# Batch 0 handed from stage to stage on the chip, and weights converted in finer steps

## The chip, the cores and the metric

The kernel runs on one core of a Trainium2 chip. The metric is the device time of one execution in microseconds (us). The engines of the core work in parallel, each through its own queue in order: TensorE (PE) multiplies matrices, VectorE (DVE), ScalarE (ACT) and GpSimd (POOL) work on elements, SyncE (SP) issues transfers (DMAs); ACT and POOL issue transfers too. PEld is PE's weight load, which is the operand that stays in the array. PE writes to an accumulator memory of eight banks (PSUM), which DVE and ACT read.

## The reference

Two blocks follow each other. The first filters the sequence of each batch and channel in the frequency domain, the second is a two-layer network without bias. `x` is 8 x 3008 x 256 in float32. The two weight matrices come as float64.

```python
X = np.fft.rfft(x, axis=1)
Y = X * (filt_r + 1j * filt_i)[None, :, :]
y = np.fft.irfft(Y, n=x.shape[1], axis=1).astype(np.float32)
h = y.reshape(24064, 256) @ w_in          # 256 x 2048
g = h - np.tanh(h)
out = (g @ w_out).astype(np.float32)      # 2048 x 256
```

## The kernel before

**The transform.** 3008 is 64 x 47, and the transform over it is done as products with constant matrices, in three stages per batch. The first stage (`first0` for batch 0, `first` for the others) multiplies 24 pairs of rows of x with `f`: for each pair r, f[r] is the operand that stays in the array and x, 256 channels wide, moves through it. The results are written to a scratch tensor `ct1[b]` in memory and read back in another order by `load_a2`, for the middle stage: that one goes over seven slots (`SLOTS`, five frequencies of 24 rows each, and a last one of two). Per slot it forms two products (`forth`, lines 279 to 294), multiplies by the filter on DVE (`filtered`, 296 to 313), forms the products back (`back`, or `back0` for batch 0), and writes them to a second scratch `ct2[b]`. The last stage (`last`, line 410) reads `ct2` as `e2`, multiplies with `g`, and yields 128 channels x up to 512 tokens, transposed, in `ut`.

**The dense part.** Tokens go in 48 groups (8 batches of 6), the 2048 hidden columns in four quarters: that makes 192 rounds U, four for a group. Round U issues `up(U)` (the product with the quarter of `wu`), in between the steps of `shrink(U - 1)` (h - tanh h, by three ACT activations and DVE products) and of `down(U - 2)` (the product with `wd`). Both products are done in two-by-two blocks with seven products in place of eight, so seven forms of each weight block are kept (`wu` and `wd`, [128, 7, 1024]), of which some are differences (`sums`, line 198, four subtractions on POOL), and the moving operands need differences too: `combine` (line 432), four subtractions, on POOL for nearly all rounds. The round's four sums in h are made on DVE (lines 476, 493, 501, 509), three copies between them on ACT (line 459). The first group of a batch has 448 tokens, so its rounds have 224 columns in place of 256.

**The weights.** float64 cannot be computed with, so each weight is loaded as a pair of 32-bit words (`raw`) and put together again as float32 from its bits. A job (`converted`, line 134) is 128 x 512 numbers; a quarter of `wu` or of `wd` is two jobs and one `sums`. A job is three operations of DVE on the upper word (it, pt, st: mantissa, exponent, sign), two of ACT (ft, pt), one multiply-add with the lower word, the cap of the exponent at 255, the shift into place, and two or three products that write the forms. It is a generator that stops after the load and at four other places. Quarters 0, 1 and 2 of `wu` (six jobs, loaded by POOL's queue) are converted ahead of the dense part, four of the jobs after the first stage of batch 0 and two after its last slot; the other five quarters (wd 0, wu 3, wd 1, 2, 3) in the first dense rounds by `weights_slow`, loaded by SP's queue two jobs ahead, two steps at each of the five calls of `t` in a round.

**The order around the change.** All instructions are in an order written by hand. Before the dense part: the loads of x of batch 0 (SP) and of `f` and `mats` (ACT), the filter rows by POOL (`filters_of`), a small copy `gate` on POOL that waits for the second part of x, and behind it on POOL's queue the loads of the first weights. In the dense part a plan (`planned`, line 937) gives positions to the steps of the transform of the next batches: position 20c + 5u + k is call k of `t` in quarter u of group c. In the first batch `first(1)` is spread over positions 6 to 20, `first(2)` over 20 to 34 (`LEAD`), `middle(1)` over 34 to 104 (`LAG`). `middle` begins with its own loads of a2 and ft, issued when its first step comes. SP's queue also issues the 48 stores of each group's result (`store`, `store_some`).

## Time and profile before

| | us |
|---|---|
| median of 3 runs (2797.88 to 2799.99) | 2798.9 |
| the profiled execution | 2804.2 |
| its span, first to last instruction | 2802.3 |
| PE busy in the span | 2702.2 |
| DVE, ACT, POOL busy | 1682.9, 1735.9, 1375.7 |

The slices on the page are 70 us wide. The first dense round begins at 106.27 us, round 10 at 287.82 us. A record of PE in this float32 kernel is half a matmul: a product is two records. The busy time of an engine says little where its rounds have different limits, so the first 300 us are best read by stretches; from then on PE is busy throughout.

### The profile page before, as it was taken

The page shows a single profiled execution, that of the slowest core. Times are in us where ns is not written, and L with a number is a line of the kernel's source. Part 1 is how long each engine was busy: PE and PEld are TensorE (multiplying, and loading weights), DVE is VectorE, ACT ScalarE, POOL GpSimd, SP SyncE. Part 2 cuts the span into 40 slices and gives each one's busy share as a digit, 9 for nine tenths or more (in the row PEclk, how much of TensorE's full clock was granted, in tenths as well). Part 3 has the DMA queues.
Part 4 walks back from the last instruction along what each step waited for, and adds up shares of the span by engine and source line. Part 5 has one row for each costly group of instructions (what it writes and reads, how often), then busy time and mean ns, then how long its engine had stood idle before and what let it go on. Part 6 is the DMA issues. An engine that isn't in the chain of part 4 may idle for free.

```text
span 2802.3 us, 36449 instructions
## 1 busy us (share of the span) xinstructions
PE 2702.2 (96%) x12878; PEld 2375.4 (85%) x12878; DVE 1682.9 (60%) x2076; ACT 1735.9 (62%) x2603; POOL 1375.7 (49%) x1184
## 2 busy tenths in 40 slices
PE   4888999999999999999999999999999999999998
PEld 3677888988889888988889888898888988899886
DVE  4864775666556665656656666566654766554544
ACT  2455666666666666666666666666666666666665
POOL 4355555544445454545455444454544554454452
PEclk8989999999999999999999999999999999999999
DMA  8655323323132332233223331242322222111110
GB/s 235 196 172 143 76 46 84 86 69 83 50 95 75 88 82 59 69 76 103 55 62 74 102 85 47 61 115 66 78 53 69 53 64 54 30 24 33 21 26 18
DMA packets 341378, 215.44 MB, mean 77 GB/s; under 512 B 227736, under 2 KB 300988, under 8 KB 340995
## 3 DMA queue, kind: packets, MB, share of 16 engines
q1 hardware_dynamic: 295740, 151.00, 22.8%
q10 hardware_dynamic: 40071, 52.71, 6.0%
q0 software_dynamic: 5376, 9.33, 1.2%
q8 instruction: 103, 1.69, 0.2%
q14 instruction: 88, 0.72, 0.1%
HBM read 137.83 MB, written 78.12 MB: 77 GB/s over the span
## 4 chain that ended last, share of the span: by engine, by line
PE 89%; DVE 6%; issue 2%; ACT 2%; DMA 1%; SPq 0%; ACTq 0%; POOL 0%; DVEq 0%
PE o L578 38%; PE x L453 22%; PE z L453 11%; PE y L453 5%; PE pa L287 3%; PE pe L322 3%; PE pu L419 3%; PE pf L255 2%; DVE h L534 1%; DVE h L476 1%; DVE h L509 1%; DMA x<-in_x_dram 1%; DVE xy L312 0%; DVE xy L311 0%; PE pe L803 0%
## 5 line engine op out<-in xcount | busy, mean ns | idle before, releaser
L578 PE MATMUL o<-t,wd 128*128 128x256 f32 (+1 forms) x3072 | 776.5, 375 | 0.0
L433 POOL TENSOR_TENSOR t<-h 128x512 f32<-128x512 f32 (+1 forms) x190 | 261.3, 1375 | 883.9 <-DVE h L534 858.8
L534 DVE TENSOR_TENSOR h<-h,y 128x1024 f32<-128x1024 f32 (+1 forms) x384 | 512.9, 1336 | 287.2 <-ACT y L530 286.7
L578 PEld LDWEIGHTS o<-t,wd 128*128 128x128 f32 x3072 | 584.1, 190 | 70.1 <-issue 2.4
L453 PE MATMUL x<-tu,wu 128*128 128x256 f32 (+1 forms) x2304 | 586.1, 377 | 7.0 <-ACT u L459 6.7
L578 PE MATMUL o<-h,wd 128*128 128x256 f32 (+1 forms) x2304 | 584.3, 376 | 3.0 <-DVE h L534 3.0
L453 PEld LDWEIGHTS x<-tu,wu 128*128 128x128 f32 x2304 | 430.9, 190 | 68.5 <-ACT u L459 15.7
L578 PEld LDWEIGHTS o<-h,wd 128*128 128x128 f32 x2304 | 434.8, 191 | 55.0 <-DVE h L534 4.2
L459 ACT COPY s<-x 128x512 f32<-128x512 f32 (+1 forms) x192 | 110.8, 577 | 508.8 <-PE x L453 497.7
L524 ACT ACTIVATE y<-h 128x1024 f32<-128x1024 f32 (+1 forms) x384 | 400.1, 1042 | 12.8 <-ACT a L256 5.6
L527 ACT ACTIVATE y<-y 128x1024 f32<-128x1024 f32 (+1 forms) x384 | 399.2, 1040 | 12.6 <-ACT a L256 0.4
L530 ACT ACTIVATE y<-y 128x1024 f32<-128x1024 f32 (+1 forms) x384 | 399.9, 1041 | 4.6
L493 DVE TENSOR_TENSOR h<-z,u 128x512 f32<-128x512 f32 (+1 forms) x192 | 130.1, 677 | 267.8 <-ACT u L459 266.6
L459 ACT COPY u<-x 128x512 f32<-128x512 f32 (+1 forms) x384 | 219.3, 571 | 87.8 <-PE x L453 66.2
L435 POOL TENSOR_TENSOR t<-h 128x512 f32<-128x512 f32 (+1 forms) x190 | 271.9, 1431 | 0.0
L434 POOL TENSOR_TENSOR t<-h,t 128x512 f32<-128x512 f32 (+1 forms) x190 | 264.6, 1393 | 14.9
L436 POOL TENSOR_TENSOR t<-t,h 128x512 f32<-128x512 f32 (+1 forms) x190 | 267.6, 1409 | 0.0
L501 DVE COPY h<-x 128x512 f32<-128x512 f32 (+1 forms) x192 | 130.4, 679 | 159.5 <-PE x L453 158.9
L453 PE MATMUL x<-ut,wu 128*128 128x256 f32 (+1 forms) x768 | 195.8, 378 | 1.1 <-DVE h L501 1.1
L453 PE MATMUL z<-tu,wu 128*128 128x256 f32 (+1 forms) x768 | 196.3, 378 | 0.0
L453 PE MATMUL z<-ut,wu 128*128 128x256 f32 (+1 forms) x768 | 195.6, 377 | 0.0
L453 PE MATMUL y<-ut,wu 128*128 128x256 f32 (+1 forms) x768 | 194.9, 376 | 0.0
(118 smaller groups left out, 3068.6 us busy)
## 6 DMA issues: line engine op xcount, KB each, us to landing
e<-ct SPq DMA_DIRECT2D x48, 512.0 KB, 4.2
a<-ct SPq DMA_DIRECT2D x48, 480.0 KB, 5.3
ct<-e ACTq DMA_DIRECT2D x96, 240.0 KB, 2.7
ct<-a ACTq DMA_DIRECT2D x84, 256.0 KB, 2.8
x_sb<-in_x_dram SPq DMA_DIRECT2D x161, 128.0 KB, 3.4
ft<-filt SPq DMA_DIRECT2D x42, 480.0 KB, 6.7
out_dram<-ot SPq DMA_DIRECT2D x1248, 16.0 KB, 1.5
gt<-g SPq DMA_DIRECT2D x48, 256.0 KB, 2.8
```

The lines of the kernel that those rows point to most:

```text
L433: by.tensor_sub(t[0], b[0][1], b[0][0])
L434: by.tensor_sub(t[1], b[1][1], t[0])
L435: by.tensor_sub(t[2], b[1][1], b[0][1])
L436: by.tensor_sub(t[3], t[1], b[1][0])
L453: nc.tensor.matmul(bank[:, k], wu[:, q - 1, (2 * u + k) * 128:(2 * u + k + 1) * 128], rhs[q - 1], start=(first and k == 0), stop=True, ski ...
L459: ACT.copy(t, X)
L501: V.tensor_copy(h[:, 2, :, 0:w], X)
L524: ACT.activation(y[k], ht[k], AF.Arctan, scale=TURN)
L527: ACT.activation(y[k], y[k], AF.Tanh, scale=BEND)
L530: ACT.activation(y[k], y[k], AF.Square, scale=SCALE, accum_out=y_sums[:, 2 * U + k // 2:2 * U + k // 2 + 1])
L534: V.tensor_mul(ht[k], ht[k], y[k])
L578: nc.tensor.matmul(product(q), wd[:, q - 1, (2 * u + k) * 128: (2 * u + k + 1) * 128], rhs[q - 1][:, k], start=(u == 0 and k == 0 and q == ...
```

## The change

Batch 0 no longer passes through `ct1`. Its first products are formed with the two operands exchanged, so that the result has channels on the partitions; ACT copies them into `turnt`, a view of the still empty `wd`. `across` then brings a slot into the layout of the middle stage by eight transposes on PE (product with the identity `one`) and two ACT copies. The identity is loaded early and kept, not in the last round.

The conversion has a stop after each operation; the cap is made by ACT (255 minus the rest, capped at zero from below, and turned back by an exclusive-or), and `sums` is on DVE. Ahead of the dense part the first two weight loads are issued before the filter rows, the next two right after the gate; two jobs are converted before and between the first products, four steps in each slot, the rest behind the last slot. The late quarters begin four loads at a time, a job's first six steps standing ahead of the last steps of the job before; four steps at each `t` and three at each `e`, so 32 in a round. While late weights are pending, `combine` is on DVE. `first(1)` is spread over 2 to 18, `first(2)` over 18 to 34, and `middle(1)` is begun (its first loads issued) at position 27.

```diff
-    def converted(tiles, src, dsts, queue, alone=False):
+    def converted(tiles, src, dsts, queue):
...
         V.tensor_scalar(out=it, in0=hi, scalar1=0xFFFFF, scalar2=None, op0=ALU.bitwise_and)
+        yield
         V.tensor_scalar(out=pt, in0=hi, scalar1=20, scalar2=0x7FF,
                         op0=ALU.logical_shift_right, op1=ALU.bitwise_and)
-        V.tensor_scalar(out=st, in0=hi, scalar1=-2 ** 31, scalar2=None, op0=ALU.bitwise_and)
-        yield
...
+        yield
+        V.tensor_scalar(out=st, in0=hi, scalar1=-2 ** 31, scalar2=0x7F800000,
+                        op0=ALU.bitwise_and, op1=ALU.bitwise_or)
+        yield
+        ACT.activation(ft, it, AF.Identity, bias=1.0, scale=2.0 ** -20)
+        yield
+        ACT.activation(pt, pt, AF.Relu, bias=exp_b)
+        yield
+        ACT.activation(pt, pt, AF.Relu, bias=cap_b, scale=-1.0)
         yield
         V.scalar_tensor_tensor(out=ft, in0=lo, scalar=2.0 ** -52, in1=ft,
                                op0=ALU.mult, op1=ALU.add)
-        V.tensor_scalar_min(pt, pt, 255.0)
         yield
         V.scalar_tensor_tensor(out=pt, in0=pt, scalar=23, in1=st,
-                               op0=ALU.logical_shift_left, op1=ALU.bitwise_or)
+                               op0=ALU.logical_shift_left, op1=ALU.bitwise_xor)
         pt = pt.bitcast(F32)
         for cols, dst, sign in dsts:
+            yield
...
-        G.tensor_sub(w[:, 4], w[:, 6], w[:, 3])
-        G.tensor_sub(w[:, 5], w[:, 4], w[:, 0])
-        G.tensor_sub(w[:, 2], w[:, 1], w[:, 5])
-        G.tensor_sub(w[:, 6], w[:, 0], w[:, 6])
+        for to, one_in, less in ((4, 6, 3), (5, 4, 0), (2, 1, 5), (6, 0, 6)):
+            V.tensor_sub(w[:, to], w[:, one_in], w[:, less])
+            yield
...
+    def late_weights(tiles, quarters):
+
+        jobs = parts_of(quarters)
+        began = [begun(tiles, job) for job in jobs[:4]]
+        yield
+        for k in range(len(jobs) + 1):
+            if k < len(jobs):
+                for _ in range(6):
+                    next(began[k])
+                    yield
+            if k:
+                yield from began[k - 1]
+                if k + 3 < len(jobs):
+                    began.append(begun(tiles, jobs[k + 3]))
+                if k % 2 == 0:
+                    yield from sums(quarters[k // 2 - 1])
+        pending.clear()
...
-        combine(b, [tu[:, k, 0:w] for k in range(4)], G if i else V)
+        combine(b, [tu[:, k, 0:w] for k in range(4)], V if pending else G)
...
-                G if U + 2 < 4 * len(groups) else V)
+                V if pending or U + 2 >= 4 * len(groups) else G)
...
             def first0(xt, c):
 
-                for i in range(2):
-                    r = 8 * c + 4 * i
...
-                            nc.tensor.matmul(pf[:, k], f0[:, r + 2 * j + k],
-                                             xt[:, 4 * i + 2 * j + k], start=True, stop=True)
-                        ACT.copy(a1[:, 2 * j:2 * j + 2, :], pf)
...
-                    ACT.dma_start(dram(ct1[0], r * DM, [[NH * DM, 128], [1, 4 * DM]]), a1)
-                    yield
+                for i in range(4):
+                    r = 8 * c + 2 * i
+                    pf = z0("pf", [128, 2, 2, 128])
+                    for h in range(2):
+                        for k in range(2):
+                            nc.tensor.matmul(pf[:, h, k], xt[:, 2 * i + k, h * 128:h * 128 + 128],
+                                             f0[:, r + k], start=True, stop=True)
+                    ACT.copy(turnt[:, :, :, r:r + 2], pf.rearrange("p h k n -> p h n k"))
+
+            def across(g):
+
+                a, s = SLOTS[g]
+                n = s * NH
+                t = tr.tile([KM, 4, DM], F32, tag="a2", bufs=2, name="a2")
+                for v in (1, 0):
+                    pq = z0("pq", [128, 2, DM])
+                    for k in range(2):
+                        at = (2 * v + k) * NA + a
+                        for h in range(2):
+                            nc.tensor.transpose(
+                                pq[0:n, k, h * 128:h * 128 + 128],
+                                turnt[:, h, at:at + s].rearrange("p a r -> p (a r)"), one)
+                    ACT.copy(t[0:n, 2 * v:2 * v + 2], pq[0:n])
+                return t
...
-                    e1 = tr.tile([KM, 2, DM], F32, tag="e1", bufs=2, name="e1")
+                    e1 = pro.tile([KM, 2, DM], F32, tag="e1", bufs=3, name="e1")
...
+            ACT.dma_start(one, one_d)
             ACT.dma_start(mats, mats_d)
...
+            jobs = parts_of(range(3))
+            began = [begun(tiles0, job, queue=G) for job in jobs[:2]]
             fts = {0: filters_of(0)}
...
-            jobs = parts_of(range(3))
-            began = [begun(tiles0, job, queue=G) for job in jobs[:2]]
+            began += [begun(tiles0, job, queue=G) for job in jobs[2:4]]
             fts[1] = filters_of(1)
-            began += [begun(tiles0, job, queue=G) for job in jobs[2:4]]
...
-            for c in range(3):
-                for _ in first0(xs[c], c):
-                    pass
-            a2 = {0: load_a2(0, 0), 1: load_a2(0, 1)}
-            next(began[0])
-            for k in range(4):
-                convert(k)
+            convert(12)
+            first0(xs[0], 0)
+            convert(14)
+            first0(xs[1], 1)
+            first0(xs[2], 2)
+            a2 = {0: across(0), 1: across(1)}
...
-                    a2[g + 2] = load_a2(0, g + 2)
+                    a2[g + 2] = across(g + 2)
...
                 if g < last_g:
+                    convert(4)
                     back0(g, nn)
...
-                f = [spread(NX, *((6, 20) if b == 1 else (20, LEAD) if b == 2
+                f = [spread(NX, *((2, 18) if b == 1 else (18, LEAD) if b == 2
...
                     next(dw, None)
+                    for _ in range(3):
+                        next(late, None)
...
+                    if i == 1 and pos == LEAD - 7:
+                        mids[1] = middle(1, z1)
+                        next(mids[1])
...
-                    next(late, None)
-                    next(late, None)
+                    for _ in range(4):
+                        next(late, None)
```

More of the change, by code (lines that the diff above doesn't have):

```diff
@@ L119 @@
     exp_b = cst.tile([128, 1], F32, name="exp_b")
+    cap_b = cst.tile([128, 1], F32, name="cap_b")
     groups = [(b, c) for b in range(BATCH) for c in range(NC)]
     count = cst.tile([1, 1], I32, name="count")
+    one = cst.tile([128, 128], F32, name="one_sb")
     def ways(g, back):
@@ L835, with convert @@
             G.tensor_copy(gate, xs[1][0:1, 0, 0:1])
[L836 to L837 removed]
+            began += [begun(tiles0, job, queue=G) for job in jobs[2:4]]
             fts[1] = filters_of(1)
[L839 removed]
             turned_rows()
[L842 to L859 removed]
+            early = weights(tiles0, range(3), G, began)
+            next(early)
+            def convert(n):
+                for _ in range(n):
+                    next(early, None)
+            convert(12)
[4 more added lines that the diff above has]
+            a2 = {0: across(0), 1: across(1)}
             last_g = len(SLOTS) - 1
@@ L890 @@
                     next(fs)
-                    late = weights_slow(tiles1, (4, 3, 5, 6, 7))
+                    signs.clear()
+                    late = late_weights(tiles1, (4, 3, 5, 6, 7))
                     next(late)
             e2s[0] = load_e2(*groups[0])
-            for k in range(4, len(jobs)):
-                convert(k)
+            convert(100)
             warm = z0("warm", [128, 2, 128])
@@ L1007 @@
                     if U == total - 1:
-                        one = tr.tile([128, 128], F32, tag="x", bufs=3, name="one_sb")
-                        nc.sync.dma_start(one, one_d)
                         ones = cst.tile([128, 1], F32, name="ones")
```

84 lines of the change are left out of this document (42 added, 42 removed).

## The prediction

> **What bounds the kernel now.** I read the page first, then the busy time by stretch, then the timeline and the chain of the first 110 us, and last the waits of the first dense rounds.
>
> ```profile
> span 2802.3 us, 36449 instructions
> PE 2702.2 (96%) x12878; PEld 2375.4 (85%) x12878; DVE 1682.9 (60%) x2076; ACT 1735.9 (62%) x2603; POOL 1375.7 (49%) x1184
> PE   4888999999999999999999999999999999999998
> PEclk8989999999999999999999999999999999999999
> ```
>
> A slice is 70 us. From the fifth on PE is full at full clock, and the diff removes no matmul there: 2,500 us are out of reach. What can move lies in the first 260 us. The next two fences are rows of busy time by stretch: start and end, length, then busy time and count for PE, PEld, DVE, ACT and POOL, the granted clock, the DMA share and GB/s. First the stretches before the dense part:
>
> ```profile
> 20.00:30.00 10.00, 8.98 (x34) 7.25 (x33) 0.00 (x0) 2.95 (x6) 5.09 (x9) 1.00 1.07 257
> 30.00:52.69 22.69, 7.20 (x27) 5.48 (x25) 17.07 (x35) 9.36 (x16) 7.90 (x10) 0.70 0.86 289
> 52.69:95.07 42.38, 34.15 (x140) 26.00 (x140) 37.85 (x46) 9.96 (x17) 23.60 (x38) 0.92 0.79 216
> ```
> ```profile
> 40.00:50.00 10.00, 2.29 (x6) 1.80 (x7) 9.86 (x20) 2.82 (x5) 4.23 (x5) 0.50 0.84 234
> ```
> ```profile
> 58.41:64.62 6.21, 6.21 (x15) 4.80 (x16) 5.49 (x7) 0.59 (x1) 6.21 (x12) 0.52 0.53 145
> 64.62:86.00 21.38, 21.27 (x98) 17.04 (x97) 18.11 (x22) 7.04 (x12) 12.00 (x23) 1.00 0.95 247
> ```
>
> Until 30 us the DMA engines are full (share 1.07) and DVE does nothing at all. From 30 to 52.69 DVE converts weights, from 40 to 50 with 9.86 of 10 us busy; from 52.69 to 95.07 it is busy 37.85 of 42.38 us (5.4 per slot) with the filter of batch 0. In the last two rows, parts of the same stretch, PE has no gap: its clock is 0.52 at first, then 1.00, at 21.27/98 = 0.217 us a record. The chain and the timeline say the same:
>
> ```profile
> 2.02 16.12 DMA x<-in_x_dram
> ```
> ```profile
> 28.53 3.69 PE L778 MATMUL pf<-x,f 128*128 128x256 f32 x16 [1.02 <-DMA x<-in_x_dram]
> 40.17 0.42 DVE L145 TENSOR_SCALAR conv<-raw 128x512 int32<-128x512 int32 x1
> 43.64 0.42 DVE L145 TENSOR_SCALAR conv<-raw 128x512 int32<-128x512 int32 x1
> 47.71 5.19 PE L287 MATMUL pa<-a,mats_sb 120*120 120x256 f32 x16 [15.49 <-issue]
> 52.69 0.68 DVE L292 TENSOR_TENSOR xy<-pa,xy 120x512 f32<-120x512 f32 x1
> 94.39 0.68 DVE L312 TENSOR_TENSOR xy<-nn 48x512 f32<-48x512 f32 x1
> 104.45 1.97 PE L419 MATMUL pu<-gt,e 128*128 128x128 f32 x16
> ```
>
> The last part of x lands at 28.5; the round trip through memory ends at 47.7; the filter begins at 52.69, held by DVE's four conversions; 104.45 is the last product before dense round 0. Second fence, one row per dense round, U0 to U6:
>
> ```profile
> 106.27:118.50 12.23, 7.17 (x30) 5.34 (x29) 10.94 (x26) 4.39 (x8) 3.65 (x6) 0.88 0.31 89
> 118.50:133.48 14.98, 11.01 (x41) 8.74 (x41) 11.56 (x22) 9.74 (x16) 4.89 (x8) 0.87 0.67 203
> 133.48:156.26 22.78, 17.55 (x73) 15.82 (x73) 18.00 (x28) 13.98 (x24) 13.90 (x17) 0.85 0.56 169
> 156.26:178.14 21.88, 17.62 (x86) 16.42 (x85) 17.23 (x26) 12.62 (x21) 12.59 (x13) 0.84 0.47 155
> 178.14:201.82 23.68, 18.90 (x77) 16.58 (x77) 16.01 (x21) 11.42 (x19) 13.66 (x17) 0.86 0.62 196
> 201.82:217.74 15.92, 15.92 (x77) 14.33 (x76) 6.80 (x11) 11.06 (x18) 7.03 (x10) 1.00 0.74 222
> 217.74:242.83 25.09, 18.38 (x77) 15.54 (x76) 6.21 (x8) 10.79 (x16) 13.75 (x15) 0.85 0.73 187
> ```
>
> U5 is what PE needs with the same 77 matmul records as U4 and U6: 15.92 us, no gap, clock 1.00. U0 to U4 take 95.55 us and are set by DVE (73.74 us busy, 77%), which converts the late weights there. U6 has another cause, in the waits and the timeline:
>
> ```profile
> PE pa L287 <- DMA a<-ct: 6.7, 1, 6.7
> PE pf L255 <- DVE h L476: 13.4, 4, 4.8
> DVE h L493 <- ACT u L459: 12.6, 6, 4.8
> DVE ft L160 <- ACT ft L157: 8.6, 4, 3.8
> ```
>
> **Part 1, before the dense part.** Removed: six stores of 512 KB on ACT's queue, seven loads on SP's, and the wait of SP and PE for them. Added: 56 transposes and 14 ACT copies. First products are turned round (x stationary, 128 columns moving): 96 records in place of 48. Moved: two weight loads (0.5 MB each) ahead of x's end on POOL's queue, past the filter loads of slot 0; two more ahead of those of slot 1. The prices:
>
> ```profile
> L649 PE MATMUL pt<-one_sb,o 128*128 128x128 f32 x8 | 1.5, 286 | 0.1
> L436 DVE TENSOR_TENSOR tu<-tu,ut 128x224 f32<-128x224 f32 x1 | 0.4, 379 | 0.0
> L780 ACT COPY a<-pf 128x512 f32<-128x512 f32 x12 | 6.7, 587 | 25.1 <-PE pf L778 18.1 <-DMA ct<-a 7.0
> L158 ACT ACTIVATE conv<-conv,exp_b 128x512 int32<-128x512 int32 x6 | 4.3, 709 | 0.2 <-DVE conv L146 0.2
> L164 DVE SCALAR_TENSOR_TENSOR pt<-pt,st 128x512 int32<-128x512 int32 x10 | 9.9, 989 | 0.2
> L534 DVE TENSOR_TENSOR h<-h,y 128x896 f32<-128x896 f32 x8 | 9.0, 1121 | 0.7 <-ACT y L530 0.7
> L476 DVE TENSOR_TENSOR h<-y,s 128x448 f32<-128x448 f32 x4 | 2.4, 610 | 0.0
> ```
>
> x's end: 1.05 MB more in a full stretch, at 257 GB/s, is 4.1 us; nothing, if it only takes turns with what competed before. I take 3.5, since POOL's loads already ran beside x after 20 us: x ends at 32. Then 32 records of 128 columns at 1.97/16 = 0.12 us: 4 us; copy 0.6; 16 transposes at 0.19 (1.5/8): 3 us; half a slot's product, its copy and semaphores some 2: the filter begins near 42 (36 with x unmoved and half of this overlapped; 47 with a cold clock), against 52.69. But jobs 2 and 3 are now converted between the slots: 18 DVE operations of 24 steps. One job without the dropped cap is 43.64 - 40.17 = 3.47 less 0.35, 3.1 us; two jobs, four subtractions at 0.38 (the row has 224 columns, I take it for 256) and the start of job 4 (0.7) are 8.4, less the 0.7 of job 2 that runs before the slots: 7.7. The slots then take 42.4 + 7.7 = 50 us, the filter ends at 92 instead of 95.07, and what follows it (104.45 - 95.07 = 9.4 us to the last product) stays. PE gets 8 x 0.19 = 1.5 us per slot on top of 24 records at 0.217 (5.2): 6.7, about what DVE then has, 5.4 + 1.3: a tie. Of DVE's 4.5 us of idleness in this stretch (42.38 less 37.85) I count 2 as filled, as the stores get three buffers in place of two and the conversions stand in the gaps. **Gain 5, between -1** (PE sets the pace after a cold start, 6 us lost) **and 12.** First products' extra cost is inside this sum; ACT's added copies (3 us per slot in all) hide under the 6.7, and would cost their 0.6 each without it. POOL loses 12 subtractions; the four queued loads behind it gain, not lose.
>
> **Part 2, U0 to U4.** Ten jobs remain. Removed from DVE: ten caps (0.35), now on ACT at 0.71. Moved from POOL to DVE: 20 subtractions, the combines of U1 to U3 (4 of 448 columns at 0.61 each) and one small combine in U3. Gone with POOL's work is its disturbance: L164 took 989 ns as a mean in these rounds, where the six before 107 us took 693:
>
> ```profile
> L164 DVE SCALAR_TENSOR_TENSOR conv<-conv 128x512 int32<-128x512 int32 x6 | 4.2, 693 | 0.2
> ```
>
> DVE's work for U0 to U3: conversions 10 x 3.2 = 32; subtractions 20 x 0.33 = 6.6 (0.38 less an estimated 0.05, since operations in a row overlap, as do the seven or eight that fill 3.47 us of a job); combines 12 x 0.58 = 7; small ones 2.6; 16 sums at 0.57 and 6 products (L534) at 1.08 = 15.6. Total 64. The finer steps (four per quarter and three per call between, 32 a round; 128 in all) finish it by the end of U3, and U4 is left to PE at U5's 15.9, or 15.7. DVE's busy share decides: 77% as now gives 64/0.77 + 16 = 99 (3.5 lost); 68% (the worst round now, U4: 16.01 of 23.68) gives 110 (14.5 lost); 98% gives 81 (14 won). The wait of L160 for ACT (8.6 us) goes, since a job's ACT steps now lie a job ahead; L493's wait for the copy chain stays in part, as that copy is queued behind three ACT steps that need DVE. I take 86%: 64/0.86 + 16 = 90.4. **Gain 5, between -15 and 14.** ACT, 52.2 us busy in U0 to U4, gets 7 more and does not bind. Batch 1's first products move from positions 6-20 to 2-18: nothing in DVE-bound rounds, 0.3 us in U5.
>
> **Part 3, U6.** Loads for batch 1's middle are issued at position 27 instead of with their first use at 34.
>
> ```profile
> 232.36 0.46 SPq L270 DMA_DIRECT2D a<-ct  x1
> 239.30 2.03 PE L287 MATMUL pa<-a,mats_sb 120*120 120x256 f32 x4 [6.71 <-DMA a<-ct]
> 241.12 1.91 PE L453 MATMUL z<-ut,wu 128*128 128x256 f32 x4
> ```
>
> 7 positions are 1.4 rounds, 22 us; from issue to first use it is 6.9. The wait of 6.7 goes, and the slow matmuls after it (1.91 us for four, where L419's sixteen of half the width took 1.97). U6 becomes U5's 15.9, 9.2 less; the slow clock reaches past its end, where I estimate 0.8. **Gain 10, between 0** (SP is held before position 27 by a buffer) **and 11.** What is late next would be the following slot's load, issued at 34 and used ten positions later. The identity's early load (64 KB) costs under 0.3.
>
> Sum: 5 + 5 + 10 = 20 us. The profiled execution took 2804.2 (span 2802.3), 5.3 above the median 2798.9; taken from the median, the forecast is 2779.
>
> **Rivals.** *DVE becomes the wall* (slower): 20 subtractions and three combines lie in front of sums that PE waits for (13.4 us already). At 55% busy U0 to U4 take 64/0.55 + 16 = 132, 37 lost: 2799 + 37 - 15 = 2821. It decides below 64% (100 + 16 = 116, 20.6 lost against 15 won elsewhere), where the kernel is 5.6 us slower; that 0.2% is about what a measurement can tell from no change. For: more DVE work in four rounds than in any now. Against: 68% is the worst round and 89% U0. *DVE stays nearly full*: 12 + 14 + 10 = 36, 2763. For: the 98% of 40 to 50 us. *The prefetch hides nothing*: 10 lost, 2789. Against: the queue is calm at position 27, the stores of group 0 come later. *Rounds lose as at 68%, the rest holds*: 2798, no change. *PE stays throttled in the slots* (0.52 in the stretch from 58.41): at that clock a slot's 24 records take 10.3 us instead of 5.2; five slots more at it cost 26: 2805. Against: matmuls outnumber transposes 24 to 8 there. Beside it, the Trainium skill ("TensorE: Matmul & The Clock Gate", Part 4: PE-mode transpose) says that transposes take some 275 ns and do not count as PE activity for the clock; by its price the 56 would cost 15.4 us, not the 10.6 of the row of L649, and the gain 15 instead of 20; whether they lower the clock among matmuls no row here shows.
>
> **Numbers.** Forecast (gain 10 to 30) 0.52; DVE nearly full 0.16; prefetch for nothing 0.06; no change 0.12; wall 0.09; throttled 0.05. Faster: the first three and a third of the fourth, 0.78; slower: the wall and, since its 26 may come in part, 0.02 of the throttled, 0.11; the rest, 0.11, within 0.2%. Range 2762 to 2799: from the full-DVE case to no change; the wall's and the throttled slots' ends stay out.
>
> **What would show it.** First filter operation near 42 and not 52.69; last product before round 0 near 100; no load or store of batch 0 through the first scratch; U0 to U3 with DVE above 85% and POOL nearly idle, U4 near 16; no wait for `a` in U6. Wrong, if DVE falls under 64% there, if first products wait longer for L476, or if PE's clock stays near 0.5 in the slots.

## The result and the profile after

The changed kernel takes 2769.8 us (median; 2767.8 to 2771.5) against 2799.1 for the kernel before: 29.3 us less, a ratio of 0.9895 with a 95% interval of 0.9878 to 0.9913. The forecast was 2779, with a range of 2762 to 2799: the sign and the range held, the gain was half as large again as the 20 us forecast. The profiled execution shown here took 2767.8 (span 2766.0), 2.0 below its median, where that of before was 5.3 above the 2798.9 of its own runs. So the two traces differ by 36.4 us where the medians differ by 29.3; some 7 us of what the traces show is scatter between executions and not the change.

The page after, the four lines that answer to those of before:

```profile
span 2766.0 us, 36630 instructions
PE 2695.2 (97%) x12982; PEld 2373.7 (86%) x12982; DVE 1674.8 (61%) x2109; ACT 1755.4 (63%) x2633; POOL 1328.8 (48%) x1136
PE   6799999999999999999999999999999999999998
PEclk9899999999999999999999999999999999999999
```

PE is full from the third slice on instead of the fifth. In the 2,500 us behind, which the change leaves as they were, the two traces differ by some 3 us. Busy time by stretch before the dense part (start and end, length, then busy time and count of PE, PEld, DVE, ACT and POOL, granted clock, DMA share, GB/s):

```profile
20.00:30.00 10.00, 9.63 (x62) 9.44 (x62) 1.60 (x4) 5.91 (x8) 5.19 (x9) 1.00 1.06 215
30.00:38.69 8.69, 7.61 (x59) 7.14 (x60) 0.76 (x3) 6.28 (x10) 3.52 (x5) 1.00 0.92 260
38.69:83.81 45.12, 38.83 (x186) 30.34 (x184) 43.89 (x63) 19.34 (x34) 18.51 (x34) 0.96 0.63 183
83.81:95.33 11.52, 11.03 (x44) 7.83 (x42) 7.08 (x17) 5.51 (x9) 0.00 (x0) 0.73 0.41 131
```

The filter of batch 0 runs from 38.69 to 83.81, and DVE is busy 43.89 of these 45.12 us (97%): it took the conversions in almost without a gap. Parts of the same stretch:

```profile
44.00:50.00 6.00, 6.00 (x33) 5.14 (x32) 5.81 (x10) 2.79 (x6) 4.88 (x9) 1.00 0.58 157
50.00:56.00 6.00, 6.00 (x33) 5.20 (x32) 5.86 (x9) 3.32 (x7) 3.43 (x7) 1.00 0.56 150
...
72.00:78.00 6.00, 4.88 (x19) 2.86 (x18) 5.86 (x11) 1.16 (x2) 0.00 (x0) 0.87 0.66 194
```

In the first slots, where the transposes are, PE has no gap either and its clock is full; later, without transposes, PE has gaps and only DVE is full. The timeline from 30 us on gives the prices:

```profile
30.20 3.81 PE L815 MATMUL pf<-f,x 128*128 128x128 f32 x32 [0.57 <-DMA f<-f]
34.89 1.96 PE L829 MATMUL pq<-one_sb,wd 128*120 128x128 f32 x16 [0.89 <-ACT wd L817]
38.42 1.04 PE L829 MATMUL pq<-one_sb,wd 128*120 128x128 f32 x8
...
43.55 0.66 PE L852 MATMUL pe<-nn,mats_sb 120*120 120x256 f32 x2 [2.37 <-DVE nn L331]
...
93.51 1.97 PE L442 MATMUL pu<-gt,e 128*128 128x128 f32 x16 [0.49 <-DMA e<-ct]
```
```profile
38.69 0.69 DVE L315 TENSOR_TENSOR xy<-pa,xy 120x512 f32<-120x512 f32 x1 [5.24 <-PE pa L310]
```

The last first products start at 30.20, sixteen transposes take 1.96 us, and 93.51 is the last product before round 0 (104.45 before). The dense rounds, U0 to U6, and a row for U0 to U3 together:

```profile
95.33:107.27 11.94, 9.67 (x39) 7.81 (x39) 10.54 (x27) 8.77 (x15) 6.93 (x12) 0.86 0.35 96
107.27:126.02 18.75, 11.72 (x46) 8.75 (x44) 12.61 (x29) 13.07 (x22) 4.51 (x8) 0.91 1.03 326
126.02:142.87 16.85, 14.79 (x73) 13.49 (x73) 15.86 (x34) 13.78 (x24) 0.00 (x0) 1.00 0.65 208
142.87:163.16 20.29, 15.67 (x86) 14.31 (x85) 17.95 (x41) 14.48 (x24) 0.00 (x0) 1.00 0.43 132
163.16:180.06 16.90, 15.16 (x72) 13.68 (x73) 10.22 (x18) 9.67 (x15) 0.37 (x1) 1.00 0.53 175
180.06:195.47 15.41, 15.06 (x74) 13.58 (x73) 6.89 (x11) 9.88 (x16) 7.22 (x10) 1.00 0.84 231
195.47:211.01 15.54, 15.54 (x73) 13.65 (x72) 6.21 (x8) 10.67 (x16) 7.93 (x10) 1.00 0.48 149
```
```profile
95.33:163.16 67.83, 51.85 (x239) 44.36 (x238) 56.96 (x128) 50.10 (x82) 11.44 (x19) 0.95 0.64 198
```

U6 is now 15.54 us without a gap in PE at full clock, where it was 25.09. U0 to U4 take 84.7 instead of 95.55 (some 4 us of the difference lie in U0 to U3, some 7 in U4), and DVE is busy 56.96 of 67.83 us in U0 to U3 (84%). The main waits that are left there, of 95.33 to 163.16 (engine, line, what it waited for, then total, times, longest):

```profile
DVE h L516 <- ACT u L482: 8.2, 4, 5.6
PE x L476 <- ACT u L482: 6.6, 5, 1.8
PE pf L278 <- DMA x_sb<-in_x_dram: 2.5, 1, 2.5
PE pf L278 <- DVE h L499: 2.4, 1, 2.4
```

L516 is line 493 of before, L499 is line 476, and PE's L476 is line 453. Three of these waits before, in its U0 to U3 (106.27 to 178.14 us):

```profile
PE pf L255 <- DVE h L476: 8.7, 3, 4.3
PE x L453 <- ACT u L459: 6.3, 4, 3.0
DVE h L493 <- ACT u L459: 4.1, 3, 2.3
```

PE's wait for the sums fell from 8.7 to 2.4, the conversion's own wait for ACT (8.6) is gone, and DVE's wait for the copy chain grew from 4.1 to 8.2. PE's own wait for ACT's copies of u, now its largest in these rounds, stayed as it was (6.3 and 6.6).

**Where the time went.** For all runs below I took from the traces, for each round, the start of ACT's first copy `s` in it (it lies some 1 us behind the round's first product). Three sums from it serve throughout: the start of round 0, the length of U0 to U4, and that of U5 to U8. Before: 107.3, 95.6, 72.0. After: 96.4, 84.7, 60.8. That is 10.9 + 10.8 + 11.2 = 32.9 us; the rest of the 36 comes behind them, nearly all after round 90, and is scatter. How much of the 10.9 and 10.8 is scatter too can be judged from experiments that leave a part of the program as it was: with the old prologue round 0 starts at 107.3, 109.7 and 105.6 (mean 107.5), with the new one between 96.4 and 98.3 in six executions (mean 97.4); U0 to U4 take 95.6, 93.1 and 92.2 with the old conversion (mean 93.6; the last two are the experiments on the kernel before, below) and 84.7 to 86.8 with the new one in four (mean 86.1). So the three parts are worth about 10, 7.5 and 11 us, some 29 together, which is what the medians say (29.3). The totals of single runs are less exact: the kernel before had medians from 2799.1 to 2800.8 from one measurement to the next, and the ratio's interval of every run below 2780 touches or overlaps that of the changed kernel, though no execution of the runs from 2774.8 up was as fast as the changed kernel's slowest. Where a difference is small, the argument goes by the rounds in the traces.

### The profile page after: what moved, and what is told of

It reads as the page before. It is cut to its first block, busy times and chain, and to the rows that moved or that the text cites. A ratio compares the mean times of both kernels' runs of the same rounds, so it can differ in the third digit from the quotient of the medians.

```text
span 2766.0 us, 36630 instructions
## 1 busy us (share of the span) xinstructions
PE 2695.2 (97%) x12982; PEld 2373.7 (86%) x12982; DVE 1674.8 (61%) x2109; ACT 1755.4 (63%) x2633; POOL 1328.8 (48%) x1136
## 4 chain that ended last, share of the span: by engine, by line
PE 88%; DVE 5%; DMA 2%; ACT 2%; issue 2%; POOL 0%; ACTq 0%; DVEq 0%; SPq 0%; POOLq 0%
PE o L601 38%; PE x L476 22%; PE z L476 11%; PE y L476 5%; PE pe L345 3%; PE pa L310 3%; PE pu L442 3%; PE pf L278 2%; DVE h L557 1%; DMA x<-in_x_dram 1%; DVE h L532 1%; DVE h L499 1%; DMA filt<-in_filt_r_dram 0%; DVE xy L335 0%; DVE nn L326 0%
## 5 line engine op out<-in xcount | busy, mean ns | idle before, releaser
L456 POOL TENSOR_TENSOR t<-h 128x512 f32<-128x512 f32 (+1 forms) x187 | 257.7, 1378 | 939.4 <-DVE h L557 916.2
L476 PE MATMUL x<-tu,wu 128*128 128x256 f32 (+1 forms) x2304 | 586.6, 377 | 7.6 <-ACT u L482 7.1
L476 PEld LDWEIGHTS x<-tu,wu 128*128 128x128 f32 x2304 | 430.6, 190 | 69.9 <-ACT u L482 17.4
L516 DVE TENSOR_TENSOR h<-z,u 128x512 f32<-128x512 f32 (+1 forms) x192 | 130.0, 677 | 269.8 <-ACT u L482 268.6
L458 POOL TENSOR_TENSOR t<-h 128x512 f32<-128x512 f32 (+1 forms) x187 | 267.5, 1431 | 0.0
L476 PE MATMUL x<-ut,wu 128*128 128x256 f32 (+1 forms) x768 | 194.1, 375 | 2.2 <-DVE h L524 2.2
L476 PE MATMUL z<-ut,wu 128*128 128x256 f32 (+1 forms) x768 | 194.6, 376 | 0.0
L476 PE MATMUL z<-tu,wu 128*128 128x256 f32 (+1 forms) x768 | 194.6, 376 | 0.0
L476 PE MATMUL y<-ut,wu 128*128 128x256 f32 (+1 forms) x768 | 193.7, 375 | 0.0
```

Of the source, the lines that this page charges most:

```text
L456: by.tensor_sub(t[0], b[0][1], b[0][0])
L458: by.tensor_sub(t[2], b[1][1], b[0][1])
L476: nc.tensor.matmul(bank[:, k], wu[:, q - 1, (2 * u + k) * 128:(2 * u + k + 1) * 128], rhs[q - 1], start=(first and k == 0), stop=True, ski ...
```

## The experiments

The theory was that of the prediction, corrected by the trace: three nearly separate gains, of the hand-over, of the conversion in U0 to U4, and of the loads at position 27. Diffs are against the changed kernel unless it says against the kernel before.

### Without the early loads of the middle stage

```diff
-                    if i == 1 and pos == LEAD - 7:
-                        mids[1] = middle(1, z1)
-                        next(mids[1])
```

> The changed kernel, but the first loads of batch 1's middle are again issued with its first step. Theory (the prefetch hides one load): a wait of some 6.7 us for `a` comes back in U6, with a cold clock behind it, and nothing moves before U6; 9.5 to 11 us longer than the changed kernel, ratio to before about 0.993. Rival (SP is calmer there in the changed kernel, since the plan of the first products is shifted, so the load lands in time anyway): under 3 us longer.

Measured: 2779.1 us, ratio 0.9924 (0.9911 to 0.9938), 9.2 above the changed kernel. U5 to U8 take 69.9 instead of 60.8, of which U6 24.3, and the wait of before is back (waits of this kernel, 195 to 232 us):

```profile
PE pa L310 <- DMA a<-ct: 5.9, 1, 5.9
```

In the changed kernel no such wait is left. The part is worth some 9 us there, a little under the 9.5 to 11 of the theory.

### The early loads alone, put into the kernel before

Against the kernel before, the three lines above are added.

```diff
+                    if i == 1 and pos == LEAD - 7:
+                        mids[1] = middle(1, z1)
+                        next(mids[1])
```

> The kernel before with nothing but the early issue of those loads at position 27. Theory: 9.5 to 11 us faster than before (ratio 0.9962), all of it in U6 and U7. Rival (it needs the late weights out of the way, which now hold the two load buffers longer): SP is held at position 27 and the wait moves to an earlier round; under 4 us faster.

Measured: 2795.5 us, ratio 0.9985 (0.9976 to 0.9994), only 5.3 less than the kernel before. U6 is 16.4 instead of 26.0, but U5, which holds the new loads, is 20.6 instead of 15.9. The timeline of U5:

```profile
216.48 0.58 ACT L459 COPY u<-x 128x512 f32<-128x512 f32 x1 [3.33 <-DMA ft<-filt]
...
217.12 1.66 PE L453 MATMUL x<-tu,wu 128*128 128x256 f32 x4 [2.95 <-ACT u L459]
```

ACT stood 3.3 us; it had ended a copy of batch 2's first products (they stand at positions 20 to 34 here) at 213.16 (212.57 + 0.59) and issued their store only at 216.12. PE waits 2.95 behind it and loses its clock (0.63 from 218 to 222). DMA share from 214 to 218 is 1.00. So neither expectation was met, and the wait did not move to SP's buffer: a store on ACT's queue comes late, and ACT's copies for the dense part stand behind it. What the store waits for comes out two runs further on.

### The early loads and the shifted first products, in the kernel before

```diff
-                f = [spread(NX, *((6, 20) if b == 1 else (20, LEAD) if b == 2
+                f = [spread(NX, *((2, 18) if b == 1 else (18, LEAD) if b == 2
...
+                    if i == 1 and pos == LEAD - 7:
+                        mids[1] = middle(1, z1)
+                        next(mids[1])
```

> The kernel before with the early issue of the middle's loads and with the first products at positions 2 to 18 and 18 to 34. Theory (the early loads cost 4.6 us in U5 when the first products stand denser around them, as the two runs with the old positions show: 20.6 and 19.9 us instead of 15.5; with the new positions that stall is not met): U5 and U6 take 15 to 16 us each, and the whole is 9 to 13 us faster than before, ratio near 0.996. Rival (U5 is short in the changed kernel for its late weights' sake): U5 stays near 20 and the gain near the 5 us of the early loads alone.

Measured: 2790.4 us, ratio 0.9965 (0.9951 to 0.9978): 10.2 us less than the kernel before, twice the gain of the loads alone. U5 is 16.0 and U6 14.9. The shift of the first products, which the prediction valued at 0.3 us, is worth some 5 once the loads are early.

### The old positions of the first products, in the changed kernel

```diff
-                f = [spread(NX, *((2, 18) if b == 1 else (18, LEAD) if b == 2
+                f = [spread(NX, *((6, 20) if b == 1 else (20, LEAD) if b == 2
```

> The changed kernel with the first products of batches 1 and 2 at positions 6 to 20 and 20 to 34 as before. Theory (PE has slack in U0 to U3 and none from U4 on): the shift gained, U0 to U3 shorter by less than U4 to U6 get longer, 1 to 4 us longer in sum. Rival (U1, 20.1 us where it took 15.7 before, pays for products that begin before their x is there): U1 3 to 5 us shorter and U0 to U6 as long or shorter in sum.

Measured: 2774.8 us, ratio 0.9913 (0.9897 to 0.9928), 4.9 above the changed kernel. U0 to U3 take 67.6 (67.9 in the changed kernel), U4 to U6 take 54.0 instead of 47.8. The timeline of U5 has the same two rows as the kernel before with the loads:

```profile
195.60 0.59 ACT L482 COPY u<-x 128x512 f32<-128x512 f32 x1 [2.85 <-DMA ft<-filt]
...
196.24 2.08 PE L476 MATMUL x<-tu,wu 128*128 128x256 f32 x4 [2.45 <-ACT u L482]
```

The same loss in both kernels, by the same two rows: the shift is a condition of the early loads. Why the store waits for `ft`, though it needs nothing of it, can be read from the semaphores that the traces keep. A landing transfer counts up a semaphore. The transfers of SP's and ACT's queues share eight of them in turn, and in these traces none of their 2,300 transfers was issued before the one that last had its semaphore had landed. So a slow load holds back the transfer that comes to its semaphore next, whatever queue that stands in:

| kernel | `ft` load issued | landed | next transfer with its semaphore | issued |
|---|---|---|---|---|
| before, loads early | 208.41 | 216.04 | ACT's store of a first product | 216.12 |
| changed, old positions | 186.56 | 195.16 | ACT's store of a first product | 195.24 |
| before, loads early, shift | 202.41 | 211.08 | SP's load of x | 211.10 |
| changed kernel | 185.31 | 194.27 | SP's load of x | 194.29 |

In all four the load takes 7.6 to 9.0 us and the next transfer goes out within 0.1 us of its landing. With the old positions that is a store on ACT's queue, and ACT's copies, for which PE waits, stand behind it; with the shift it is a load on SP's queue, and ACT goes on. The shift does not keep the first products apart from the loads (those of batch 2 still run beside them, with ACT's stores at 187.77 and 193.04 in the changed kernel): it changes whose turn it is. No run moves the semaphore alone.

### Batch 0 through memory again, the conversions as changed

```diff
-                    pf = z0("pf", [128, 2, 2, 128])
...
-                    ACT.copy(turnt[:, :, :, r:r + 2], pf.rearrange("p h k n -> p h n k"))
+                        pf = z0("pf", [128, 2, DM])
...
+                        ACT.copy(a1[:, 2 * j:2 * j + 2, :], pf)
+                    ACT.dma_start(dram(ct1[0], r * DM, [[NH * DM, 128], [1, 4 * DM]]), a1)
...
-                            nc.tensor.transpose(
...
+                return load_a2(0, g)
```

> The changed kernel, but batch 0 goes through memory again (old first products, six stores, seven loads; no transposes); the identity is loaded in the last round as before. Theory (both parts of the start count, the hand-over by PE and the conversion under the loads of x): the filter begins some 9 us later, at 47 to 48 instead of 38.7, the slots lose 1.5 us of PE work each but DVE sets their pace, and round 0 begins 7 to 9 us later than in the changed kernel (95.3). Rival (the round trip was hidden behind conversions, which alone held the filter until 52.7): round 0 begins within 3 us of the changed kernel's.

Measured: 2786.1 us, ratio 0.9952 (0.9938 to 0.9965), 16.2 above the changed kernel. Round 0 starts at 110.0, 13.6 later than in the changed kernel, and no sooner than in the three executions with the old prologue. DVE's timeline:

```profile
53.36 0.69 DVE L314 TENSOR_TENSOR xy<-pa,xy 120x512 f32<-120x512 f32 x1 [20.67 <-PE pa L309]
```

The round trip through memory still ends the wait for the filter, at 53.36; DVE stands 20.7 us before it, and the conversions that it did there in the kernel before now stand between the slots, where they cost time. The loss is larger than the theory had it: conversions between the slots are no gain by themselves.

### The hand-over alone, the first conversions as before

```diff
-            jobs = parts_of(range(3))
-            began = [begun(tiles0, job, queue=G) for job in jobs[:2]]
             fts = {0: filters_of(0)}
...
-            convert(12)
-            first0(xs[0], 0)
-            convert(14)
-            first0(xs[1], 1)
-            first0(xs[2], 2)
+            for c in range(3):
+                first0(xs[c], c)
             a2 = {0: across(0), 1: across(1)}
+            convert(48)
...
-                    convert(4)
                     back0(g, nn)
```

> The changed kernel, but the weights ahead of the dense part are loaded and converted as before: loads behind the gate and behind each other's filter rows, four jobs between the first products and the first slot, none in the slots. Theory (neither the hand-over nor the early conversion is worth anything alone: either the memory or DVE holds the filter until about 50): the filter begins at 47 to 51 instead of 38.7, the slots take some 40 us, round 0 begins at 102 to 105 instead of 95.3. Rival (the hand-over alone carries the gain): round 0 within 3 us of 95.3.

Measured: 2779.4 us, ratio 0.9923 (0.991 to 0.9937), 9.6 above the changed kernel. The filter begins at 50.17, because DVE has four jobs to convert first, and round 0 starts at 105.7. The stretch of the filter, and DVE's only wait in it:

```profile
50.17:92.50 42.33, 34.92 (x169) 28.49 (x170) 36.61 (x45) 13.87 (x25) 15.28 (x28) 0.90 0.54 156
```
```profile
DVE xy L315 <- PE pa L310: 4.6, 4, 2.2
```

Slots are 6.05 us apart (42.33 by seven) with DVE idle for 5.7 of 42.3 us: here PE, with its transposes, sets the pace. The cap stays on ACT here and the subtractions on DVE, so this is the hand-over with the old order of loads and conversions. Together with the run before this makes a square: old prologue 107.5 (mean of three), conversions moved alone 110.0, hand-over alone 105.7, both 97.4 (mean of six). Each half by itself moves round 0 by no more than old prologues differ among themselves; the ten microseconds come from the two together. The hand-over empties the time in front of the filter only if DVE has no conversions to do there, and the conversions can go between the slots at a profit only if the slots begin sooner.

### Subtractions and combines back on POOL

```diff
-            V.tensor_sub(w[:, to], w[:, one_in], w[:, less])
+            G.tensor_sub(w[:, to], w[:, one_in], w[:, less])
...
-        combine(b, [tu[:, k, 0:w] for k in range(4)], V if pending else G)
+        combine(b, [tu[:, k, 0:w] for k in range(4)], V if not i else G)
...
-                V if pending or U + 2 >= 4 * len(groups) else G)
+                V if U + 2 >= 4 * len(groups) else G)
```

> The changed kernel, but the weight subtractions and the combines of the first rounds are on POOL again. Theory (POOL's work disturbs DVE): L165's mean in U0 to U3 rises from 682 ns to 900 or more, DVE stays as busy as it is although it has 12 us less to do, and U0 to U4 are 3 to 10 us longer than 84.7. Rival (DVE's work is what counts): DVE's operations keep their durations and U0 to U4 get 5 to 12 us shorter.

Measured: 2770.2 us, ratio 0.9894 (0.9879 to 0.9909): no difference to the changed kernel, and U0 to U4 take 83.9. DVE's groups in U0 to U3 (count, then busy time and mean ns of one), of the changed kernel and then of this one:

```profile
L165 DVE SCALAR_TENSOR_TENSOR pt<-pt,st 128x512 int32<-128x512 int32 x10 | 6.8, 682 | 0.0
...
L148 DVE TENSOR_SCALAR conv<-raw 128x512 int32<-128x512 int32 x10 | 4.3, 434 | 0.1
...
L150 DVE TENSOR_SCALAR pt<-raw 128x512 int32<-128x512 int32 x10 | 4.2, 419 | 0.0
```
```profile
L165 DVE SCALAR_TENSOR_TENSOR pt<-pt,st 128x512 int32<-128x512 int32 x10 | 7.3, 734 | 0.0
L150 DVE TENSOR_SCALAR pt<-raw 128x512 int32<-128x512 int32 x10 | 7.3, 727 | 0.0
L148 DVE TENSOR_SCALAR conv<-raw 128x512 int32<-128x512 int32 x10 | 7.0, 698 | 0.2
```

DVE is rid of the subtractions and combines and yet as busy in U0 to U3, 57.9 us instead of 57.0, since its own operations take longer while POOL works: L150 727 ns instead of 419, L148 698 instead of 434. The two effects cancel, and neither expectation was met: the theory had the rounds 3 to 10 us longer and L165 at 900 ns, where it has 734. Which engine has this work made no difference, so it cannot be the source of the gain in U0 to U4. The Trainium skill ("SBUF — State Buffer", section "Who interferes with whom") has DVE and POOL contend for a shared pair of ports, and counts `tensor_scalar` among the operations that can; the rows of L150 and L148 agree with it.

### The cap back on DVE

```diff
-        V.tensor_scalar(out=st, in0=hi, scalar1=-2 ** 31, scalar2=0x7F800000,
-                        op0=ALU.bitwise_and, op1=ALU.bitwise_or)
+        V.tensor_scalar(out=st, in0=hi, scalar1=-2 ** 31, scalar2=None, op0=ALU.bitwise_and)
...
-        ACT.activation(pt, pt, AF.Relu, bias=cap_b, scale=-1.0)
+        V.tensor_scalar_min(pt, pt, 255.0)
...
-                               op0=ALU.logical_shift_left, op1=ALU.bitwise_xor)
+                               op0=ALU.logical_shift_left, op1=ALU.bitwise_or)
```

> The changed kernel with the cap of the exponent on DVE again (ten operations of 0.42 us in the late rounds), not as a third step of ACT (ten of 0.71). Theory (after the pool run: DVE's work does not set U0 to U3, the chain of copies through ACT does): U0 to U4 0 to 4 us shorter than 84.7, since the copies of u stand behind less on ACT. Rival (DVE's work sets the pace): 2 to 4 us longer.

Measured: 2778.9 us, ratio 0.9926 (0.9913 to 0.994), 9.1 above the changed kernel; U0 to U4 take 92.2, 7.5 more, and round 0, with the cap in the prologue's jobs too, starts at 99.0. DVE's group for the cap:

```profile
L159 DVE TENSOR_SCALAR pt<-pt 128x512 int32<-128x512 int32 x10 | 4.3, 433 | 11.4 <-ACT pt L157 11.2
```

The cap's 4.3 us are the smaller part: in front of it DVE stands 11.2 us for ACT. Some of it is paid back (the wait of 8.2 at L516 is no longer among DVE's in U0 to U3), and 7.5 remain. Neither expectation had this size.

### One job at a time instead of one job ahead

```diff
-                for _ in range(6):
-                    next(began[k])
-                    yield
-            if k:
-                yield from began[k - 1]
-                if k + 3 < len(jobs):
-                    began.append(begun(tiles, jobs[k + 3]))
-                if k % 2 == 0:
-                    yield from sums(quarters[k // 2 - 1])
+                yield from began[k]
+                if k + 4 < len(jobs):
+                    began.append(begun(tiles, jobs[k + 4]))
+                if k % 2:
+                    yield from sums(quarters[k // 2])
```

> The changed kernel with each late job's last steps straight behind its first six, not behind those of the next job. Theory (a job ahead takes away DVE's wait for ACT): DVE waits 6 to 10 us for ACT at L162 in U0 to U4 as it did before (8.6), and they are 3 to 8 us longer than 84.7. Rival (DVE has that time to spare, since it waits 8.2 us for the copies of u instead): the wait at L516 shrinks by as much, U0 to U4 within 2 us.

Measured: 2776.0 us, ratio 0.9911 (0.9898 to 0.9925), 6.1 above the changed kernel; U0 to U4 take 90.3, 5.6 more. Of DVE's waits from 98 to 170 us:

```profile
DVE conv L162 <- ACT conv L156: 6.2, 3, 5.8
DVE pt L165 <- ACT pt L160: 5.2, 5, 2.8
```

The first is line 160 of before, whose wait of 8.6 the prediction said would go. It returns with the old order, and a wait for the cap on ACT comes to it: 11.4 us together, about as much as the 11.2 that DVE waited for ACT with the cap on DVE.

### Fewer steps a round, and coarser steps

First, three steps instead of four at each `t` (27 a round instead of 32, so the conversion ends later):

```diff
-                    for _ in range(4):
+                    for _ in range(3):
                         next(late, None)
```

> The changed kernel with 27 late steps a round in place of 32 (three at each `t`): the same operations in the same fine order, ending at 4.7 rounds instead of 4.0, as they did before. Theory (it is the earlier end that frees U4): U4 goes back from 16.9 to 19 to 22, U1 and U3 gain less than that, U0 to U4 are 1 to 5 us longer than 84.7. Rival (it is the fine order that gained, the end does not matter): U0 to U4 within 1 us or shorter, since U0 to U3 have less to do.

Measured: 2768.2 us, ratio 0.9887 (0.9872 to 0.9902). U3 is 16.8 and U4 19.2 where they were 20.0 and 16.8; the sum is 84.3 instead of 84.7. Then all steps in five lumps a round:

```diff
-                    for _ in range(3):
-                        next(late, None)
...
-                    for _ in range(4):
+                    for _ in range(7 if k % 2 else 6):
                         next(late, None)
```

> The changed kernel with its 32 late steps a round in five lumps of 6 or 7 at `t` and none at `e`. Theory (the earlier end): U0 to U4 within 2 us of 84.7. Rival (fine steps): the sums of h stand behind lumps of 3 to 4 us, PE waits for L499 as before (13 us instead of 2.4), U0 to U4 are 4 to 10 us longer.

Measured: 2771.3 us, ratio 0.99 (0.9885 to 0.9915); U0 to U4 84.8. Neither the earlier end of the conversion nor the finer steps matter. The 1.7 us by which the first of the two lies below the changed kernel, with the same sum of rounds, also shows what two medians differ by without a cause in these rounds.

### The tile of zeros in another buffer

In U0 the loads of batch 1 on SP's queue stand behind two stores of zeros, and these wait for their tile, whose buffer a weight load holds until DVE's L162 has used it. POOL fills the tile only then, in the changed kernel:

```profile
100.34 0.53 POOL L971 MEMSET zero<- 128x512 f32 x1 [34.17 <-DVE conv L162]
```

Here the zeros get a buffer of their own that is free.

```diff
-                zero = tr.tile([128, 2 * DM], F32, tag="a2", bufs=2, name="zero")
+                zero = dn.tile([128, 2, CH * 128], F32, tag="ot", bufs=1, name="zero")[:, 0]
```

> The changed kernel with the tile of zeros for the filter copies in the result's buffer (free until U6), not in one that a late weight load holds until DVE has used it. Theory (SP stood still from 95 to 100.9 behind the stores of that tile, and the loads of batch 1's first products behind them): the loads leave 4 to 5 us earlier, the 2.5 us wait for x_sb in U1 goes, U0 to U4 2 to 4 us shorter, a version faster than both. Rival (the transfers are full there, share 1.03, so the loads land as late): within 1 us.

Measured: 2767.1 us, ratio 0.9883 (0.9868 to 0.9899), 2.7 below the changed kernel; U0 to U4 take 81.9, 2.8 less. The first store of zeros in SP's timeline, of the changed kernel and of this one:

```profile
100.90 0.89 SPq L973 DMA_DIRECT2D filt<-zero  x1
```
```profile
94.43 0.89 SPq L973 DMA_DIRECT2D filt<-zero  x1
```

It goes out 6.5 us sooner, and the wait of PE for `x_sb` (2.5) is gone. The trace shows the mechanism; the two intervals overlap, so the time alone does not prove that it beats the changed kernel. It has the lowest median of all.

## Why the prediction was right, and where it was not

The sign, and the three places of the gain, held. The sizes, predicted and found:

| part | predicted gain | this pair of traces | means over like traces |
|---|---|---|---|
| before the dense part | 5 (-1 to 12) | 10.9 | 10 |
| U0 to U4 | 5 (-15 to 14) | 10.8 | 7.5 |
| U6 and its neighbours | 10 (0 to 11) | 11.2 | 11 |

**Part 1: right in its steps, half of what was found in its sum.** Two terms were mis-sized by some 3 us each. The first is the start. x's end was put at 32; the last first products start at 30.2. Their 32 records take 3.81 us (4 predicted). A transpose was priced at 0.19, from eight in 1.5 us; sixteen in a row take 1.96 us, 0.12 each, eight 1.04. So the filter begins at 38.69, not at 42. The second is the slots: 42.4 + 7.7, less 2 us of idleness to be filled, is 48, and they take 45.12. DVE's busy time grew by 6.0 (43.89 against 37.85) and not by 7.7, and of its 4.5 us of idleness 3.3 was filled (1.2 is left). What follows the filter takes 9.7 us to the last product (9.4 predicted). The tie of PE and DVE came, at less than the 6.7 us a slot that were forecast: while there are transposes both are full (6.00 and 5.86 of the 6 us from 50 on), and with the hand-over alone, where DVE has less to do, PE sets 6.05. Over all seven slots DVE, busy 97%, has more than PE.

**The throttled slots did not come.** The granted clock is 0.96 from 38.69 to 83.81, with 40 transposes or so among 186 records: 1.00 in the slots with transposes, and below 1 (0.87 from 72 to 78) only where they are over and PE has gaps. The rival's price of 10.3 us for a slot at a clock of 0.52 was a little high, too: 5.2/0.52 is 10.0, which puts its case at 2803 and not 2805. The Trainium skill ("TensorE: Matmul & The Clock Gate", Part 4: PE-mode transpose) gives some 275 ns for one in bf16; single records here, in float32, last 272 ns as well, but in a row they follow each other every 0.12 us, so its figure is the time of one and not the price of one more. Its statement that transposes do not count as activity for the clock cost nothing here, among three times as many matmul records.

**Part 2: the total was nearer than its reasons.** 64 us of DVE work at 86% gave 90.4. The trace has 57.0 us in U0 to U3 at 84% (the sign that was named was above 85%), and U4 at 16.9, where the prediction put 16: the work does not end with U3 (DVE is busy 10.2 us in U4 against 6.9 in U5). So the share was right and the work too large by 7, half of it because it lies in U4. But three of the reasons given fell. The move of subtractions and combines from POOL, with the end of POOL's disturbance, is neutral (2770.2). The finer steps and the early end are, too (84.8 and 84.3 against 84.7). What carries most of the gain is the one sentence about waits: a job's ACT steps lie a job ahead, so DVE does not stand for ACT in the middle of a job. Taking the order away costs 5.6 us of rounds, putting an operation of DVE back straight behind the step of ACT that it needs costs 7.5; against the mean of 86.1 us these are 4.2 and 6.1 of the part's 7.5. Where the rest of it comes from no run isolates. The wait at L493 was to stay "in part"; in U0 to U3 it doubled instead (8.2 against 4.1), and that the copy is queued behind more steps of ACT, as was argued, no run here isolates. ACT did not bind (50.1 of 67.8 us). POOL was not idle in U0 and U1 (6.9 and 4.5 us), since the zeros and the filter's copies go out there, and was idle in U2 and U3.

**Part 3: right, with one term missed.** The wait for `a` and the slow clock after it are gone, 9 to 11 us. The step that failed is "batch 1's first products move from positions 6-20 to 2-18: nothing in DVE-bound rounds, 0.3 us in U5". The shift moves batch 2's as well, from 20-34 to 18-34, and those are the ones beside the early loads. Without the shift of the first products the early loads lose about 5 us in U5. The question that the prediction put for every stall, what is late next, was answered with the following slot's load; without the shift the answer is a store on ACT's queue that has to wait for the semaphore of the `ft` load.

**The rivals.** DVE as the wall is out: its share in U0 to U3 is 84%, far above the 64% at which it would decide. "Rounds lose as at 68%" is out with it, and "the prefetch hides nothing" by the run without it. "DVE nearly full" came true between 38.69 and 83.81 only; some 3 us of the underestimate lie there.

## What to carry to other kernels

Where one engine's in-order work goes over to another and back within a job, put the other's steps a job ahead: the order of the steps was worth more than half of the part here, and how finely they were cut or which of two contending engines did the rest was worth nothing that the runs show. Two changes that fill the same hole from both sides have to be valued together: the hand-over alone and the moved conversions alone each gave nothing beyond scatter, both together ten microseconds. When a load is issued earlier, look at which transfer is next to get its semaphore, and on whose queue that stands.

## What the runs showed of the hardware that was not expected

A PE transpose of 128 columns in float32, in a row of sixteen, costs 0.12 us, no more than a matmul record of the same width (32 in 3.81 us), which is half a product; the clock stays at 1.00 with 8 transposes and 24 matmul records a slot. Integer operations of DVE on one operand take 727 instead of 419 ns as a mean while POOL subtracts beside them, a larger loss here than that of the two-operand operation of L165 (734 against 682). In the kernel before, the same two-operand operation lost the more (L164, 989 against 693), and it was from there that the prediction had its price; so the loss is no fixed price of an operation. And a store on ACT's queue was issued 2.5 to 3 us late since a load of SP's queue, 7.6 and 8.6 us under way while the DMA engines were full (share 1.00 and 1.04), had the semaphore that was its turn; in both kernels where it occurred it cost the round 4 to 5 us.
